# Seven quarter products in place of eight in a part of the first projection (retention attention followed by a snake MLP)

## The chip, the cores and the metric

The kernel runs on one core of a Trainium2 chip. The time is the device time of one execution in microseconds, and of several executions the median counts.

## The reference, cut to what matters

Eight batches of eight heads (576 positions, head size 64) go through a causal, decaying retention attention without softmax; its output, 4608 tokens of 512 features, goes through an MLP with a hidden layer of 2048.

```python
scores = scale * np.matmul(q, k.transpose(0, 1, 3, 2))
ret = scores * Dmat[None]                    # Dmat: gamma[h] ** (i - j) for i >= j, else 0
x = np.matmul(ret, v)                        # then as (4608, 512)
h = x @ w_in                                 # (4608, 512) @ (512, 2048)
s = np.sin(alpha * h)
g = h + s * s / (alpha + 1e-09)
return (g @ w_out).astype(np.float32)        # (4608, 2048) @ (2048, 512)
```

## The kernel before, in words

The tokens are taken in nine blocks `n` = 0 to 8 of 512. Blocks 0 to 7 hold the first 512 positions of batch `n`; block 8 holds the last 64 positions of all eight batches ("ends"). A block's input `xs[n]` lies transposed in SBUF (128 partitions, 4 chunks of the 512 features, 512 tokens); for block 8 it is `xS`, which class `Ends` makes while block 7 is projected.

**First projection.** The hidden layer is cut into 16 units of 128 features. `project(n, u, tag)` (line 560) is four matmuls 128x128x512 into one PSUM bank; units 4 to 7 take their weights from `w_in16[1]`, a tile whose columns are laid out so that a unit's 128 columns stand four apart. Then `sine` (573) on ScalarE reads the bank, `square` (581) is done on ScalarE or VectorE, and `product` (590) on VectorE reads the bank once more and writes `g = h + s²/alpha` to `gT[n]`. Only `product` gives the bank back. There are eight banks: `h0`, `h1`, `h2` go round (`next(h)`), `m0` and `m1` are double ones, also used by the attention, and `op` is for the second projection.

**Second projection.** From block 4 on it is already done with seven products in place of eight. For block `n-1` they are spread over the units of block `n`: behind units 1, 3, 5, ... stands one of `part_product(n-1, k)` (659), 16 matmuls 128x128x256, in the order 1, 2, 6, 7, 5, 3, 4. Products 2, 7 and 3 go into the bank of 1, 6 and 5: they are added to what lies there. So `after_product` (699), which reads the bank of 1, 6 or 5 (into `low`, `mid` or the output tile `osb`), must be done before TensorE may go on into it. The sums that these products take as factors are `row_sum` S1 to S4 (644, recorded at 652), VectorE instructions 128x1024 with both inputs in SBUF, half of them behind units 13 to 15 of block `n-1`, half behind units 0 to 2 of block `n`.

**Order.** All is issued under a manual schedule: each engine runs its instructions in the order of the program text, and TensorE, ScalarE, VectorE and GpSimd wait for each other by semaphores alone. `unit_start` records `project`, `sine` and what `at_unit(u, ...)` put there; then comes the part product, if any, then `unit_end` with `square`, `product` and what `behind(u, ...)` put there. `ON_V` names the units whose square is VectorE's. In block 7, `Ends` issues its scores at unit 7, its values at unit 13 and its results (`keep`, ScalarE and VectorE) behind it; a mark (`told`, 273), an empty instruction on GpSimd, stands between two halves of the values. GpSimd does the casts and state sums of the attention for the blocks before, and nothing in blocks 7 and 8 but such marks. `PAD` = 8 small loads (`fill_up`, 746) stand in SyncE's queue at units 3 to 10 of block 7.

## Time and profile before

| | us |
|---|---|
| median of 3 runs (lowest, highest) | 295.13 (293.91, 295.16) |
| the profiled execution | 293.87 |
| its span, first to last instruction | 292.1 |
| what lies around the span (293.87 less 292.1) | 1.77 |
| busy: TensorE matmul / VectorE / ScalarE / GpSimd | 282.4 / 228.7 / 206.2 / 135.8 |
| block 7's units, 221.3 to 249.6 of the span: VectorE / ScalarE / GpSimd busy | 24.7 / 20.2 / 0 |
| block 8's units, 249.6 to 277.4 of the span: VectorE / ScalarE / GpSimd busy | 23.3 / 17.6 / 0 |

In the profile's rows a line stands for the place in the kernel that recorded the instruction (L568 is `project`, L671 `part_product`, L576 `sine`, L585 ScalarE's and L587 VectorE's or GpSimd's `square`, L592 `product`, L652 `row_sum`, L702 to L717 `after_product`). PE is TensorE's matmul side, PEld its weight loads, DVE VectorE, ACT ScalarE, POOL GpSimd, SP SyncE. In a timeline the first two columns are start and length in us; `x8` merges eight instructions; a bracket at the end gives idle time before it and who ended it.

### The profile page before, as it was taken

To read this page: it belongs to the slowest core of one execution; us is meant where nothing else is said; L and a number is where in the kernel's file an instruction comes from. 1 tells how busy PE (TensorE), PEld (TensorE's weight loads), DVE (VectorE), ACT (ScalarE), POOL (GpSimd) and SP (SyncE) were. 2 spreads that over 40 slices of the span, in tenths; PEclk is the share of its full clock that TensorE was granted. 3 is DMA by queue.
4 is the path that set the end of the run, shared out by engine and by line. 5 is a ranking of instruction groups with operands and counts; after the bars stand their busy time and mean duration, and the time that the engine had idled before them with its cause. 6 is when DMAs were issued, how large, how long until landed. Compare 5 with 4: busy or idle time off the path is not lost. (4 is left out here: it accounts for less than half of the span.)

```text
span 292.1 us, 8463 instructions
## 1 busy us (share of the span) xinstructions
PE 282.4 (97%) x3480; PEld 182.9 (63%) x3480; DVE 228.7 (78%) x336; ACT 206.2 (71%) x340; POOL 135.8 (46%) x152
## 2 busy tenths in 40 slices
PE   5889999999999999999999999999999999999994
PEld 4656555555545645455776677676767676777783
DVE  2596969888659787798977697769777987987884
ACT  2588945997595887787767986897678657865500
POOL 6694777475699566560497039803960000000000
PEclk9599999999999999999999999999999999999999
DMA  7999999999999898999968985899651102111213
GB/s 211 349 235 209 242 289 317 263 262 258 226 220 188 169 159 180 274 164 180 156 154 236 133 206 144 245 137 221 167 159 43 43 10 80 36 38 36 72 38 108
DMA packets 122775, 50.06 MB, mean 171 GB/s; under 512 B 79729, under 2 KB 120689, under 8 KB 122737
## 3 DMA queue, kind: packets, MB, share of 16 engines
q1 hardware_dynamic: 118784, 44.76, 65.5%
q0 software_dynamic: 2688, 4.19, 7.9%
q10 hardware_dynamic: 1264, 0.58, 0.8%
q8 instruction: 27, 0.44, 0.6%
q14 instruction: 12, 0.09, 0.1%
HBM read 36.75 MB, written 9.44 MB: 158 GB/s over the span
## 5 line engine op out<-in xcount | busy, mean ns | idle before, releaser
L592 DVE SCALAR_TENSOR_TENSOR gT<-ss,inva,hps 128x512 f16<-128x512 f16 x144 | 105.6, 745 | 27.3 <-ACT ss L585 23.1
L576 ACT ACTIVATE s<-hps,alpha_t 128x512 f16<-128x512 f32 x144 | 96.4, 681 | 43.2 <-PE hps L568 42.4
L568 PE MATMUL hps<-xT,w_in 128*128 128x512 f16 (+1 forms) x532 | 121.4, 371 | 0.2
L568 PEld LDWEIGHTS <-w_in 128*128 128x128 f16 x596 | 66.7, 114 | 50.0 <-issue 1.0
L585 ACT ACTIVATE ss<-s 128x512 f16<-128x512 f16 x106 | 66.6, 630 | 2.8
L605 PE MATMUL ops<-w_out,gT 128*128 128x512 f16 x192 | 46.8, 380 | 0.0
L671 PEld LDWEIGHTS <-gT 128*128 128x128 f16 x384 | 37.5, 98 | 8.3
L207 POOL TENSOR_TENSOR k<-raw,cn 128x1024 f16<-128x1024 f32 (+1 forms) x17 | 28.8, 1698 | 10.2 <-DMA raw<-in_k_dram 8.7
L671 PEld LDWEIGHTS <-S 128*128 128x128 f16 x288 | 27.7, 98 | 5.3
L605 PEld LDWEIGHTS <-gT 128*128 128x128 f16 x192 | 17.9, 98 | 20.5
L363 POOL TENSOR_TENSOR s<-kvs,cn 128x256 f16<-128x256 f32 x17 | 10.4, 612 | 39.2 <-DVE S L652 24.8
L207 POOL TENSOR_TENSOR q<-raw,cn 128x1024 f16<-128x1024 f32 x13 | 25.1, 1938 | 4.9 <-DMA raw<-in_q_dram 4.6
L671 PE MATMUL hps<-T,gT 128*128 128x256 f16 x192 | 22.9, 273 | 0.0
L671 PE MATMUL hps<-w_out,gT 128*128 128x256 f16 x192 | 22.9, 273 | 0.0
L671 PE MATMUL hps<-w_out,S 128*128 128x256 f16 x192 | 22.8, 273 | 0.0
L401 DVE TENSOR_TENSOR ret<-sc,mask 128x1024 f16<-128x1024 f32 x16 | 19.2, 1220 | 2.6 <-PE sc L389 2.5
L120 ACT CAST xT<-o 128x1024 f16<-128x1024 f32 (+1 forms) x15 | 16.5, 1130 | 2.4 <-PE o L451 2.4
L587 DVE TENSOR_TENSOR ss<-s 128x512 f16<-128x512 f16 x29 | 14.9, 517 | 2.6 <-ACT s L576 2.5
L371 POOL TENSOR_TENSOR kvs<-s,kvs 128x256 f32<-128x256 f32 x21 | 15.3, 730 | 2.8 <-DVE kvs L122 1.2
L717 DVE TENSOR_TENSOR osb<-hps,low 128x512 f32<-128x512 f32 x13 | 9.0, 692 | 9.3 <-PE hps L671 9.2
L370 POOL TENSOR_TENSOR s<-kvs,cn 128x256 f32<-128x256 f32 x21 | 13.5, 642 | 5.9 <-ACT kvs L120 5.8
L652 DVE TENSOR_TENSOR S<-gT,S 128x1024 f16<-128x1024 f16 x24 | 15.6, 688 | 0.0
(83 smaller groups left out, 273.8 us busy)
## 6 DMA issues: line engine op xcount, KB each, us to landing
raw<-in_q_dram SPq DMA_DIRECT2D x16, 512.0 KB, 5.7
out_dram<-osb SPq DMA_DIRECT2D x32, 256.0 KB, 2.7
raw<-in_k_dram SPq DMA_DIRECT2D x8, 512.0 KB, 8.8
raw<-in_v_dram SPq DMA_DIRECT2D x8, 512.0 KB, 6.1
raw<-in_v_dram SPq DMA_DIRECT2D x32, 128.0 KB, 3.1
raw<-in_k_dram SPq DMA_DIRECT2D x32, 128.0 KB, 3.1
w_in<-in_moe_w_in_dram POOLq DMA_DIRECT2D x4, 512.0 KB, 11.7
w_out<-in_moe_w_out_dram POOLq DMA_DIRECT2D x4, 512.0 KB, 13.0
```

The source lines that it names most:

```text
L120: eng.copy(d_, s_)
L207: eng.tensor_tensor(dst[:, a0:a1].rearrange("p a r t d -> p t (a r) d"), t_.rearrange("p (t a) x -> p t a x", t=2)[:, :, a0:a1].rearrange( ...
L371: nc.gpsimd.tensor_tensor(self.kvs[:, c], s32, self.kvs[:, c], ADD)
L401: nc.vector.tensor_tensor(ret.rearrange("p t (z x) -> p (t z) x", z=2)[:, :, 0:n], sc.rearrange("p t (z x) -> p (t z) x", z=2)[:, :, 0:n], ...
L568: matmul(hps_of[n, fc][0][:, cols], w_in16[fc // 4][:, a, fc % 4 :: 4], xs[n][:, a, cols], start=(a == 0 and part != 1), stop=(a == KT - 1 ...
L576: nc.scalar.activation(s_t, hps, mybir.ActivationFunctionType.Sin, bias=0.0, scale=alpha_t[:, fc : fc + 1],)
L585: nc.scalar.activation(ss_t, s_t, mybir.ActivationFunctionType.Square)
L587: eng.tensor_tensor(ss_t, s_t, s_t, MULT)
L592: nc.vector.scalar_tensor_tensor(gT[n][:, fc, :], ss_t, inva[:, fc : fc + 1], hps, MULT, ADD)
L605: matmul(ops[n, c, cols.start][:, cols], gT[n][:, fk, c * P : (c + 1) * P], w_out16[:, fk, cols], start=(fk == 0), stop=(fk == FC - 1), sk ...
L652: return eng.tensor_tensor(out_, x, y, op)
L671: matmul(acc[:, 256 * j : 256 * j + 256], lhs[:, x, 128 * j : 128 * j + 128], rhs[:, x], start=(tag is not None and j == js[0] and p == 0 ...
```

## The change

Units 4 to 7 of blocks 7 and 8 are no longer four `project` calls. The 512 features of `w_in16[1]` are cut into two halves `t` (units 4 and 5, units 6 and 7), the 512 tokens into two halves `e`, and the 512 input features into two halves. Seven `sub_product`s of four matmuls 128x128x256 each (28 in all, where there were 16 of 128x128x512) give what eight quarter products gave. For this there are new sums:

- `w_in_sum` (recorded at line 754 of the changed kernel): S1 to S4 of the weights, once, eight GpSimd instructions 128x256 behind unit 14 of block 6.
- `x_sum` (769): T1 to T4 of the block's input, four GpSimd instructions 128x512 per block; for block 7 ahead of its units, for block 8 behind unit 14 of block 7.
- `after_sub` (795 to 806): products 1 and 2 are read by ScalarE, 6, 7, 5, 3 and 4 by VectorE, into `low_x`, `mid_x` and `hsb` in SBUF (float32). Products 2, 7 and 3 go into the bank of 1, 6 and 5 here too. Units 4 and 5 are whole after product 3, units 6 and 7 after product 4.
- The sine of the four units reads `hsb`. All four squares are ScalarE's; units 4 and 5 are ended by GpSimd with two instructions each (824, 825), units 6 and 7 by VectorE's `product`.
- `ON_V` goes from (3, 5, 9, 11) to (3,) in block 7 and from (3, 5, 7, 9, 11, 13) to (11, 13) in block 8. The eight `fill_up` loads move to units 3, 8, 9 and 10, two at each; `Ends`' scores stand among the products.

```diff
+    FIRST = {
+        1: ((0, 0), (0, 0)), 2: ((0, 1), (1, 0)), 3: ("S4", (1, 1)), 4: ((1, 1), "T4"),
+        5: ("S1", "T1"), 6: ("S2", "T2"), 7: ("S3", "T3"),
+    }
...
+    def w_in_sum(g, name, eng):
+        a11, a12, a21, a22 = (w_part(g, t, k_) for t in range(2) for k_ in range(2))
+        s_ = lambda x: w_sum_of(g, x)
+        x, y, op = {
+            "S3": lambda: (a11, a21, SUB), "S2": lambda: (a22, s_("S3"), SUB),
+            "S1": lambda: (a11, s_("S2"), ADD), "S4": lambda: (a12, s_("S2"), SUB),
+        }[name]()
+        for j in range(2):
+            eng.tensor_tensor(s_(name)[:, j], x[:, j], y[:, j], op)
...
+    def x_sum(n, name, eng):
+        b11, b12, b21, b22 = (x_part(n, k_, e) for k_ in range(2) for e in range(2))
+        t_ = lambda x: x_sum_of(n, x)
+        x, y, op = {
+            "T3": lambda: (b22, b12, SUB), "T2": lambda: (t_("T3"), b11, ADD),
+            "T1": lambda: (b12, b11, SUB), "T4": lambda: (b21, t_("T2"), SUB),
+        }[name]()
+        eng.tensor_tensor(t_(name), x, y, op)
+
+    def sub_product(n, g, i, tag, first=None):
+        left, right = FIRST[i]
+        accs[n, g, i] = accs[n, g, first] if tag is None else bank(tag)
+        acc = accs[n, g, i]
...
+        for j in range(2):
+            for a in range(2):
+                matmul(
+                    acc[:, 256 * j : 256 * j + 256], lhs[:, j, a], rhs[:, a],
+                    start=(tag is not None and j == 0 and a == 0), stop=(a == 1), skip_group_check=True,
+                )
+
+    def after_sub(n, g, i):
...
+        if i == 1:
+            nc.scalar.copy(low_, acc)
+        elif i == 6:
+            nc.vector.tensor_tensor(mid_, acc, low_, ADD)
+        elif i == 7:
+            nc.vector.tensor_tensor(low_, acc, low_, ADD)
+        else:
+            t, e = {2: (0, 0), 3: (0, 1), 4: (1, 0), 5: (1, 1)}[i]
+            dst = hs[t][:, :, 256 * e : 256 * e + 256]
+            if i == 2:
+                nc.scalar.copy(dst, as_pair(acc))
+            else:
+                nc.vector.tensor_tensor(dst, as_pair(acc), as_pair(mid_ if i == 3 else low_), ADD)
...
+    def product_on_pool(n, u):
+        hps, ss_t = hps_of.pop((n, u))
+        nc.gpsimd.tensor_tensor(ss_t, ss_t, inva[:, u : u + 1].to_broadcast([P, 512]), MULT)
+        nc.gpsimd.tensor_tensor(gT[n][:, u, :], ss_t, hps, ADD)
...
-            ON_V = {4: (), 5: (), 6: (0, 15), 7: (3, 5, 9, 11), 8: (3, 5, 7, 9, 11, 13)}[n]
+            ON_V = {4: (), 5: (), 6: (0, 15), 7: (3,), 8: (11, 13)}[n]
...
+            def opening(n, g):
...
+                sub_product(n, g, 1, next(h))
+                sub_product(n, g, 6, next(h))
+                after_sub(n, g, 1)
+                after_sub(n, g, 6)
+
+            def group(g, i, between, then):
+                part(slots[i])
+                for k_ in (2, 7, 5):
+                    sub_product(n, g, k_, next(h) if k_ == 5 else None, {2: 1, 7: 6}.get(k_))
+                    after_sub(n, g, k_)
+                for f in between:
+                    f()
+                part(slots[i + 1])
+                sub_product(n, g, 3, None, 5)
+                after_sub(n, g, 3)
+                sub_product(n, g, 4, next(h))
+                after_sub(n, g, 4)
+                for f in then:
+                    f()
...
+            plain_units(0, 2, units)
+            opening(n, 1)
+            group(1, 2, between, [E[1].masked] if n == 7 else [])
+            made = rest(1, (G_, V))
+            for f in (made[0], made[2], made[1], made[4]):
+                f()
+            at_unit(8, *made[6:8])
+            behind(8, *made[8:])
+            behind(8, made[3], made[5])
+            plain_units(4, 8, units)
```

(`rest` makes the list of sines, squares and ends of units 4 to 7; `plain_units` is the loop of before, two units and a part product at a time.)

**What stands where on VectorE in block 7.** Before, from the end of unit 4 (`ss_570`) to the output of part product 5 (the `osb` row): the rows L592 end units 4, 5, 6, 7 and 8 in turn, L704 and L706 read part products 6 and 7, L499 are the masks of `Ends`.

```order
L592 SCALAR_TENSOR_TENSOR gT<-ss_570,inva,hps 128x512
L704 TENSOR_TENSOR mid<-hps,low 128x512
L587 TENSOR_TENSOR ss_546<-s_544 128x512
L592 SCALAR_TENSOR_TENSOR gT<-ss_546,inva,hps 128x512
L592 SCALAR_TENSOR_TENSOR gT<-ss_548,inva,hps 128x512
L499 TENSOR_TENSOR rets<-scs,mask 128x1024
L706 TENSOR_TENSOR low<-hps,low 128x512
L592 SCALAR_TENSOR_TENSOR gT<-ss_532,inva,hps 128x512
L499 TENSOR_TENSOR rets<-scs,mask 128x1024
L592 SCALAR_TENSOR_TENSOR gT<-ss_570,inva,hps 128x512
L717 TENSOR_TENSOR osb<-hps,low 128x512
```

Now the same stretch from the reading of quarter product 7 on (its rows L797 and L704, for quarter product 6 and part product 6, stand just ahead). L806 are quarter products 5, 3 and 4; the three L592 end units 8, 6 and 7.

```order
L799 TENSOR_TENSOR low_x<-hps,low_x 128x512
L806 TENSOR_TENSOR hsb<-hps,low_x 128x2x256
L499 TENSOR_TENSOR rets<-scs,mask 128x1024
L706 TENSOR_TENSOR low<-hps,low 128x512
L806 TENSOR_TENSOR hsb<-hps,mid_x 128x2x256
L806 TENSOR_TENSOR hsb<-hps,low_x 128x2x256
L499 TENSOR_TENSOR rets<-scs,mask 128x1024
L592 SCALAR_TENSOR_TENSOR gT<-ss_570,inva,hps 128x512
L592 SCALAR_TENSOR_TENSOR gT<-ss_546,inva,hsb 128x512
L592 SCALAR_TENSOR_TENSOR gT<-ss_548,inva,hsb 128x512
L717 TENSOR_TENSOR osb<-hps,low 128x512
```

The ends of units 4 and 5 are gone from VectorE; between the ends of unit 8 and the output of part product 5 now stand the ends of units 6 and 7, with both tensors from SBUF.

**ScalarE in block 7.** Before, from the sine of unit 4 to that of unit 9 (L576 sine, L585 square):

```order
L576 ACTIVATE s_557<-hps,alpha_t 128x512
L585 ACTIVATE ss_570<-s_557 128x512
L576 ACTIVATE s_544<-hps,alpha_t 128x512
L576 ACTIVATE s_524<-hps,alpha_t 128x512
L585 ACTIVATE ss_548<-s_524 128x512
L576 ACTIVATE s_530<-hps,alpha_t 128x512
L585 ACTIVATE ss_532<-s_530 128x512
L576 ACTIVATE s_557<-hps,alpha_t 128x512
L585 ACTIVATE ss_570<-s_557 128x512
L576 ACTIVATE s_544<-hps,alpha_t 128x512
```

Now the copies of quarter products 1 and 2 and then ten instructions up to the square of unit 7 (L811 and L819 are the sines and squares of units 4 to 7, L576 the sine of unit 8, the three L585 the squares of units 8, 6 and 7):

```order
L795 COPY low_x<-hps 128x512
L804 COPY hsb<-hps 128x2x256
L811 ACTIVATE s_557<-hsb,alpha_t 128x512
L819 ACTIVATE ss_4368<-s_557 128x512
L811 ACTIVATE s_544<-hsb,alpha_t 128x512
L819 ACTIVATE ss_4371<-s_544 128x512
L576 ACTIVATE s_524<-hps,alpha_t 128x512
L811 ACTIVATE s_530<-hsb,alpha_t 128x512
L811 ACTIVATE s_557<-hsb,alpha_t 128x512
L585 ACTIVATE ss_570<-s_524 128x512
L585 ACTIVATE ss_546<-s_530 128x512
L585 ACTIVATE ss_548<-s_557 128x512
```

The first sine of the group moved from the end of unit 4's own matmuls to behind quarter product 3, and unit 8's square to behind seven others.

**GpSimd.** Where its program ended with the last cast of block 6, the difference adds the weight sums, the sums of block 7, the ends of units 4 and 5 of block 7, and the sums of block 8 (block 8's four ends follow):

```order
+L754 TENSOR_TENSOR S_w_4120<-w_in_1_71 128x256 x2
+L754 TENSOR_TENSOR S_w_4120<-w_in_1_71,S_w_4120 128x256 x2
+L754 TENSOR_TENSOR S_w_4125<-w_in_1_71,S_w_4120 128x256 x4
+L769 TENSOR_TENSOR T_x_4134<-xT_439 128x512
+L769 TENSOR_TENSOR T_x_4134<-T_x_4134,xT_439 128x512
+L769 TENSOR_TENSOR T_x_4137<-xT_439 128x512
+L769 TENSOR_TENSOR T_x_4137<-xT_439,T_x_4134 128x512
+L824 TENSOR_TENSOR ss_4368<-ss_4368,inva 128x512
+L825 TENSOR_TENSOR gT<-ss_4368,hsb 128x512
+L824 TENSOR_TENSOR ss_4371<-ss_4371,inva 128x512
+L825 TENSOR_TENSOR gT<-ss_4371,hsb 128x512
```

All of it is new; nothing of GpSimd's earlier rows moved.

More of the change, by code (lines that the diff above doesn't have):

```diff
@@ new lines, in part, with plain_units @@
+            def part(k_):
+                if k_ is not None:
+                    part_product(n - 1, k_, None if k_ in (2, 7, 3) else "op", first={2: 1, 7: 6, 3: 5}.get(k_))
+                    after_product(n - 1, k_)
+            def plain_units(i0, i1, units):
+                for i in range(i0, i1):
+                    for u in (2 * i, 2 * i + 1):
+                        unit_start(u, units[u], aside.get(u) or next(h))
+                        if u % 2:
+                            part(slots[i])
+                        if n < 8 and u == 14:
+                            square(n, u, A_)
+                            continue
+                        if n < 8 and u == 15:
+                            product(n, 14)
+                            for f in after.get(14, []):
+                                f()
+                        unit_end(u, units[u], None if A and u == 13 else V if u in ON_V else A_)
```

104 lines of the change are left out of this document (79 added, 25 removed).

## Prediction

> **What bounds the kernel now.** The page comes first: matmuls are busy for 97% of the span, no other engine over 78%.
>
> ```profile
> PE 282.4 (97%) x3480; PEld 182.9 (63%) x3480; DVE 228.7 (78%) x336; ACT 206.2 (71%) x340; POOL 135.8 (46%) x152
> ```
>
> That is a share over the whole program, so the second view is the busy time by stretch: block 7's units (first row) and block 8's (second).
>
> ```profile
> core 0: us, PE busy (x) PEld busy (x) DVE busy (x) ACT busy (x) POOL busy (x), PEclk, DMA share, GB/s
> 221.34:249.63 28.29, 28.26 (x370) 19.88 (x369) 24.73 (x38) 20.17 (x34) 0.00 (x0) 1.00 0.15 44
> 249.63:277.42 27.79, 27.79 (x195) 19.74 (x194) 23.26 (x38) 17.59 (x29) 0.00 (x0) 1.00 0.14 48
> ```
>
> In both TensorE works without a gap, at full clock: it sets the time, and nothing here can be won but matmul time. GpSimd is empty, VectorE and ScalarE have a few us each. So two questions decide: how much matmul time goes, and whether TensorE must now wait for somebody. The third view is TensorE's timeline, which gives the price of its pieces.
>
> ```profile
> 228.29 1.89 PE L568 MATMUL hps<-xT,w_in 128*128 128x512 f16 x8
> ...
> 235.98 1.89 PE L568 MATMUL hps<-xT,w_in 128*128 128x512 f16 x8
> 237.71 1.91 PE L671 MATMUL hps<-w_out,S 128*128 128x256 f16 x16
> 239.46 1.89 PE L568 MATMUL hps<-xT,w_in 128*128 128x512 f16 x8
> ...
> 256.58 1.89 PE L568 MATMUL hps<-xS,w_in 128*128 128x512 f16 x8
> ```
>
> A group's length holds the tail of its last matmul, so the price is start to start: two units 237.71 - 235.98 = 1.73 (one unit 0.87), a part product of 16 matmuls 239.46 - 237.71 = 1.75. Units 4 and 5 start at 228.29 in block 7 and at 256.58 in block 8.
>
> **Matmul time removed.** Four units, 4 x 0.87 = 3.46, go; 28 matmuls 128x128x256 come, 28/16 x 1.75 = 3.06 (one quarter product of four: 0.44). That is 0.40 a block, **0.80 in both**, 0.3% of the time. More than this can't be won, since there is no idle TensorE time to win.
>
> **What TensorE now waits for: the bank of part product 5.** Part product 3 goes into that bank, so it waits until VectorE has written `osb` from it (L717). In the changed order that row stands behind the ends of units 8, 6 and 7, which need ScalarE's squares, and these stand behind the sines and squares of units 4 and 5, which need quarter product 3. I add this chain up from ScalarE's rows (unit 8 and 9 of block 7) and VectorE's.
>
> ```profile
> 237.05 0.69 ACT L576 ACTIVATE s<-hps,alpha_t 128x512 f16<-128x512 f32 x1 [1.63 <-PE hps L568]
> 237.76 0.63 ACT L585 ACTIVATE ss<-s 128x512 f16<-128x512 f16 x1
> 238.30 0.67 ACT L576 ACTIVATE s<-hps,alpha_t 128x512 f16<-128x512 f32 x1
> ```
>
> ```profile
> 222.81 0.68 DVE L652 TENSOR_TENSOR S<-gT 128x1024 f16<-128x1024 f16 x1
> 223.41 0.42 DVE L587 TENSOR_TENSOR ss<-s 128x512 f16<-128x512 f16 x1
> ...
> 224.52 1.29 DVE L652 TENSOR_TENSOR S<-gT,S 128x1024 f16<-128x1024 f16 x2
> ...
> 228.25 0.75 DVE L592 SCALAR_TENSOR_TENSOR gT<-ss,inva,hps 128x512 f16<-128x512 f16 x1
> 228.90 1.29 DVE L652 TENSOR_TENSOR S<-gT,S 128x1024 f16<-128x1024 f16 x2
> 230.10 0.43 DVE L587 TENSOR_TENSOR ss<-s 128x512 f16<-128x512 f16 x1
> 230.57 1.40 DVE L592 SCALAR_TENSOR_TENSOR gT<-ss,inva,hps 128x512 f16<-128x512 f16 x2
> 231.96 0.69 DVE L704 TENSOR_TENSOR mid<-hps,low 128x512 f32<-128x512 f32 x1
> ...
> 247.88 1.28 DVE L122 CAST xS<-os 128x512 f16<-128x512 f32 x2
> ...
> 251.09 0.69 DVE L652 TENSOR_TENSOR S<-gT 128x1024 f16<-128x1024 f16 x1
> ...
> 252.35 1.29 DVE L652 TENSOR_TENSOR S<-gT,S 128x1024 f16<-128x1024 f16 x2
> ...
> 256.73 1.29 DVE L652 TENSOR_TENSOR S<-gT,S 128x1024 f16<-128x1024 f16 x2
> ```
>
> A square starts 0.71 after its own sine (237.76 - 237.05), the next instruction 0.54 after a square's start (238.30 - 237.76); for two independent instructions in a row I take 0.55 too. On VectorE an end (L592) takes 0.75 and the next starts 0.65 after it (1.40 for two), a reading of PSUM (L704) takes 0.69 and the next may start 0.61 after it. A reader starts 0.20 after TensorE has issued the last matmul (unit 8 is issued at 235.98 + 0.87 = 236.85, its sine starts at 237.05). Sines from SBUF, and readings into `hsb`, have no rows; I take them at these prices, since shape and types are the same. Zero is the start of quarter product 3:
>
> - 0.20 part product 7 can be read; 0.81 `hsb` of product 3 starts behind it, 1.50 it ends.
> - ScalarE: sine 4 at 1.50, square 2.21, sine 5 at 2.75, square 3.46, sines 8, 6, 7 at 4.00, 4.55, 5.10, squares 8, 6, 7 at 5.65, 6.20, 6.74. Square 8 ends at 6.28, square 7 at 7.37.
> - VectorE: end of unit 8 at 6.28, of 6 at 6.93, of 7 at 7.58, `osb` at 8.23 to 8.92.
> - TensorE meanwhile has quarter products 3 and 4, units 8 and 9, part product 5, units 10 and 11: 2 x 0.44 + 1.73 + 1.75 + 1.73 = 6.09.
>
> So part product 3 starts at 8.92 where TensorE is free at 6.09: **a wait of 2.83 in each block, 5.66 in both**. In block 7 most of it falls already on unit 11, which takes unit 8's bank: due at 5.22, released at 7.03. In block 8 the `m` banks take every third unit and only part product 3 waits. ScalarE's work before quarter product 3 can't start sooner, and VectorE's row can't be passed: each engine keeps its order.
>
> **At the front.** Quarter product 6 takes unit 2's bank. In block 7 TensorE comes there at 228.29 + 0.44 = 228.73; the end of unit 2 is done at 228.25 + 0.75 = 229.00: wait 0.27. Then 0.44, part product 6 (1.75) and quarter product 2 (0.44) bring it to 231.63 at product 7, which needs `mid_x` read. That stands behind the end of unit 3: 230.57 + 0.65 = 231.22, ends 231.91: wait 0.28. In block 8 the row sums end at 256.73 + 1.29 = 258.02, unit 3's end takes 0.65, `mid_x` is read at 259.36, and TensorE comes at 256.58 + 0.44 + 0.44 + 1.75 + 0.44 = 259.65: no wait, 0.29 to spare. **Front: 0.55.**
>
> **GpSimd's sums and ends.** They are new; the nearest rows are these (groups by shape), and its last cast in the timeline.
>
> ```profile
> L371 POOL TENSOR_TENSOR kvs<-s,kvs 128x256 f32<-128x256 f32 x21 | 15.3, 730 | 2.8 <-DVE kvs L122 1.2
> ...
> L363 POOL TENSOR_TENSOR s<-kvs,cn 128x256 f16<-128x256 f32 x17 | 10.4, 612 | 39.2 <-DVE S L652 24.8 <-PE hps L568 12.0 <-ACT kvs L120 1.8
> ...
> L191 POOL TENSOR_TENSOR ks<-ks,cn 128x512 f16<-128x512 f32 x2 | 2.1, 1042 | 1.8 <-PE o L430 1.8
> ```
>
> ```profile
> 215.71 0.61 POOL L122 CAST vs<-ends 128x512 f16<-128x512 f32 x1
> ```
>
> Eight weight sums at 0.61 run from 216.3 to 221.2, block 7's four x sums at 1.04 to 225.4: over 3 us before quarter product 6 needs T2, so TensorE waits for none of them. But they don't run alone: a place where GpSimd worked beside such VectorE rows is at 127 us.
>
> ```profile
> 127.21 1.04 POOL L191 TENSOR_TENSOR ks<-ks,cn 128x512 f16<-128x512 f32 x1 [1.77 <-PE o L430]
> ...
> 127.46 1.34 DVE L652 TENSOR_TENSOR gT<-gT 128x1024 f16<-128x1024 f16 x1
> ...
> 128.22 1.49 POOL L191 TENSOR_TENSOR qs<-qs,cn 128x512 f16<-128x512 f32 x1
> ...
> 128.73 1.26 DVE L587 TENSOR_TENSOR ss<-s 128x512 f16<-128x512 f16 x1
> ```
>
> There a row sum took 1.34 in place of 0.68 and a square 1.26 in place of 0.42: each, started while a GpSimd instruction ran, ended about as late as if it had begun at that one's end. In block 7, S2 (222.81), the square (223.41) and S1 (224.52) meet x sums. Each may lose from nothing to a whole GpSimd instruction, 1.04; I take half, 0.52, near the 0.66 of the row sum above: 3 x 0.52 = 1.56. VectorE has no gap from there to the end of unit 2, so TensorE waits that much more at quarter product 6. In block 8 the x sums run behind the casts, from 249.2 to 253.3, and meet S2 (251.09) and S1 (252.35): 1.04 less the 0.29 to spare, 0.75. **2.31 in both.**
>
> [...]
>
> GpSimd's ends of units 4 and 5 are four instructions 128x512 in float32, 0.73 (L371) plus what 256 more elements cost, 1.042 - 0.612 = 0.43: 4 x 1.16 = 4.64, from the end of square 4 (2.84 on the chain's clock) to 7.48. The ends of units 6 and 7 read `ss` and `hsb`, both in SBUF, as row sums and squares do; unit 6's, due at 6.93, would wait till 7.48: 0.55 a block, **1.10 in both**. At 0.73 each they would be through at 5.76 and cost nothing, at twice 0.73 they cost 1.75 a block.
>
> **The rest at nothing.** VectorE loses seven squares and four ends and gets ten readings; beside the named waits it has gaps. GpSimd's mark between the halves of `Ends`' values comes behind its ends: due at about 8.92 + 1.75 + 1.73 = 12.4 on the chain's clock, GpSimd is through at 7.5. SyncE's eight loads move behind units 3 and 8 to 10; a store may go out some us later, and four `osb` buffers cover that.
>
> **Sum.** -0.80 + 5.66 + 0.55 + 2.31 + 1.10 = +8.8. On the profiled execution, 293.87 (span 292.1 and 1.77 around it), this gives **302.7**; it lies 1.26 under the median of the runs shown, and a run may fall as far above.
>
> [...]
>
> **Rivals.**
> 1. *GpSimd's sums fall between VectorE's rows.* Then 2.31 and 1.10 go: -0.80 + 5.66 + 0.55 = +5.4, 299.3. For it: few places show such a cost. Against: VectorE has no gap from 222 to 234 us.
> 2. *Contention at full price*: x sums each hold a whole instruction (3.12 and 2.83 in place of 1.56 and 0.75 with a third meeting in block 8), ends 1.75 a block: +5.41 + 5.95 + 3.50 = +14.9, 308.7.
> 3. *No wait arises, not slower.* The place is the bank of part product 5: if the chain to `osb` took 6.09 in place of 8.92, TensorE would get there just in time, and the front waits would be all that stands against the 0.80: 293.87 - 0.80 = 293.1 to 293.6. It needs ten ScalarE instructions in 2.83 less than 5.87, half of their rows' prices. That quarter products cost more than 0.44 (weights four columns apart, at most a few hundredths each) moves the sum by far less.
>
> **How the numbers follow.** Forecast 0.58, rival 1 0.22, rival 2 0.15, rival 3 0.05. The time is the forecast's, 302.7. The range holds rival 1 and most of the way to rival 2: 298.9 to 308. Within 0.5% is about what a measurement of this kernel can tell from no change; slower by more 0.95, within 0.04, faster by more 0.01, since 0.80 is all that could be won.
>
> **What would show it.** In the profile after: part product 3 of blocks 7 and 8 starting right behind an `osb` row, with TensorE idle for 2 to 4 us in all before it; row sums and squares of over 1 us while L769 runs; ten ScalarE rows without a gap behind quarter product 3. It is wrong if TensorE stays without gaps there, or if the waits lie at quarter products, for GpSimd's T sums.

## The result, and the profile after

The changed kernel takes 309.49 us (median of 4 runs, 308.36 to 310.11) where the kernel before takes 294.62 beside it: a ratio of 1.052, with a 95% interval of 1.049 to 1.054. It is slower, as forecast, but by 15 us instead of 9: the forecast was 302.7, its range ended at 308.0. The profiled execution took 309.3, its span is 307.6.

Executions differ in their first 50 us, which the change leaves alone: in the profiles of this document block 7 starts anywhere from 221.1 to 227.2 us, and in three profiles of the changed kernel itself at 221.4, 223.9 and 226.2. Below I therefore compare the **stretch** from the start of block 7's units to the end of the span: 292.10 - 221.34 = 70.76 us before, 307.6 - 221.43 = 86.17 after. The difference, 15.41, is the whole loss.

The page's first part says that TensorE is busier than before and yet fills less of the span (93% where it was 97%), with 24 matmuls more.

```profile
PE 286.7 (93%) x3504; PEld 186.3 (61%) x3504; DVE 235.4 (77%) x335; ACT 211.8 (69%) x351; POOL 161.3 (52%) x176
```

The busy time by stretch says where the loss lies; these are block 7's and block 8's units in the changed kernel.

```profile
core 0: us, PE busy (x) PEld busy (x) DVE busy (x) ACT busy (x) POOL busy (x), PEclk, DMA share, GB/s
221.43:259.11 37.68, 31.10 (x383) 22.10 (x382) 28.57 (x38) 22.63 (x39) 11.89 (x12) 0.91 0.11 33
259.11:292.87 33.76, 29.31 (x206) 21.37 (x205) 25.06 (x37) 20.55 (x35) 9.63 (x8) 0.95 0.11 40
```

Block 7 went from 28.29 to 37.68, block 8 from 27.79 to 33.76. TensorE's busy time fell short of the stretch by 6.58 and 4.45, so it waits; but it was also busy *longer* than before (31.10 for 28.26, 29.31 for 27.79) although it has less to do, and the granted clock is 0.91 and 0.95 where it was 1.00. That second loss is in no term of the forecast. TensorE's timeline of block 7 shows both.

```profile
228.37 0.60 PE L779 MATMUL hps<-xT,w_in 128*128 128x256 f16 x4
232.31 1.01 PE L779 MATMUL hps<-T_x,S_w 128*128 128x256 f16 x4 [3.34 <-DVE gT L592]
233.12 3.62 PE L671 MATMUL hps<-T,S 128*128 128x256 f16 x16
236.53 1.06 PE L779 MATMUL hps<-xT,w_in 128*128 128x256 f16 x4
237.38 1.31 PE L779 MATMUL hps<-T_x,S_w 128*128 128x256 f16 x8
...
241.02 0.60 PE L779 MATMUL hps<-xT,S_w 128*128 128x256 f16 x4
...
245.37 1.03 PE L568 MATMUL hps<-xT,w_in 128*128 128x512 f16 x4
248.41 1.02 PE L568 MATMUL hps<-xT,w_in 128*128 128x512 f16 x4 [2.02 <-DVE gT L592]
250.66 1.91 PE L671 MATMUL hps<-w_out,S 128*128 128x256 f16 x16 [1.23 <-DVE osb L717]
```

```profile
core 0: us, PE busy (x), PEclk, DMA share, GB/s
...
233.12:236.53 3.41, 3.41 (x17) 0.50 0.05 10
...
237.38:238.62 1.24, 1.24 (x9) 0.78 0.00 0
250.66:252.40 1.74, 1.74 (x16) 1.00 0.49 160
282.75:285.93 3.18, 3.18 (x17) 0.53 0.23 82
```

TensorE stands 3.34 at quarter product 6, and behind it the 16 matmuls of part product 6 take 3.41 start to start (233.12 to 236.53) in place of 1.75: the clock is 0.50 there, and full again only past 238. The two waits at the back (2.02 before unit 11, 1.23 before part product 3) come as forecast, with the clock at 1.00 behind them. In block 8 the back is one wait, and the half clock follows it:

```profile
270.49 1.03 PE L779 MATMUL hps<-T_x,S_w 128*128 128x256 f16 x8 [0.93 <-DVE mid_x L797]
...
282.75 3.34 PE L671 MATMUL hps<-w_out,S 128*128 128x256 f16 x16 [3.41 <-DVE osb L717]
285.93 1.89 PE L568 MATMUL hps<-xS,w_in 128*128 128x512 f16 x8
```

Who is late at the front, VectorE's timeline of block 7 shows, beside GpSimd's x sums:

```profile
222.89 1.68 DVE L652 TENSOR_TENSOR S<-gT 128x1024 f16<-128x1024 f16 x1
224.49 1.37 DVE L587 TENSOR_TENSOR ss<-s 128x512 f16<-128x512 f16 x1
...
226.56 2.43 DVE L652 TENSOR_TENSOR S<-gT,S 128x1024 f16<-128x1024 f16 x2
...
231.43 0.73 DVE L592 SCALAR_TENSOR_TENSOR gT<-ss,inva,hps 128x512 f16<-128x512 f16 x1
```

```profile
222.87 1.15 POOL L769 TENSOR_TENSOR T_x<-xT 128x512 f16<-128x512 f16 x1
224.10 1.48 POOL L769 TENSOR_TENSOR T_x<-T_x,xT 128x512 f16<-128x512 f16 x1
225.54 1.33 POOL L769 TENSOR_TENSOR T_x<-xT 128x512 f16<-128x512 f16 x1
226.84 1.60 POOL L769 TENSOR_TENSOR T_x<-xT,T_x 128x512 f16<-128x512 f16 x1
```

The first S2 takes 1.68 (0.68 before), the square 1.37 (0.42), S1 and S4 together 2.43 (1.29; S1 0.86 and S4 1.64), each while an x sum runs: +1.00, +0.95 and +1.14, in sum 3.09. The end of unit 2, which gives quarter product 6 its bank, starts at 231.43 in place of 228.25.

**The account.** All in us, start to start, against 0.44 for a quarter product, 1.75 for a part product and 1.73 for two units:

| | forecast | block 7 | block 8 |
|---|---|---|---|
| matmul time removed | -0.40 a block | -0.40 | -0.40 |
| front waits (quarter products 6 and 7) | 2.11 / 0.75 | 3.50 | 0.28 + 1.09 = 1.37 |
| half clock behind a wait | none | 0.37 + 1.66 + 0.41 + 0.37 = 2.81 | 3.18 - 1.75 = 1.43 |
| back waits (unit 11, part product 3) | 2.83 + 0.55 = 3.38 a block | 9.64 - 6.09 = 3.55 | 9.65 - 6.09 = 3.56 |
| sum | | 9.46 (measured 9.39) | 5.96 (measured 5.97) |

(9.64 is from quarter product 3 to part product 3, 241.02 to 250.66.) The start and the tail add 0.05. The forecast missed 6.6: the half clock 4.24, the front 1.39 and 0.62, the back 0.35.

### The profile page after: what moved, and what is told of

Same layout as the page of the kernel before. It is cut to its first block, busy times and chain, and to the rows that moved or that the text cites. A ratio compares the mean times of both kernels' runs of the same rounds, so it can differ in the third digit from the quotient of the medians.

```text
span 307.6 us, 8561 instructions
## 1 busy us (share of the span) xinstructions
PE 286.7 (93%) x3504; PEld 186.3 (61%) x3504; DVE 235.4 (77%) x335; ACT 211.8 (69%) x351; POOL 161.3 (52%) x176
## 5 line engine op out<-in xcount | busy, mean ns | idle before, releaser
L592 DVE SCALAR_TENSOR_TENSOR gT<-ss,inva,hps 128x512 f16<-128x512 f16 x136 | 99.4, 743 | 32.1 <-ACT ss L585 28.1
L568 PE MATMUL hps<-xT,w_in 128*128 128x512 f16 (+1 forms) x516 | 117.8, 371 | 2.8 <-DVE gT L592 2.0
L576 ACT ACTIVATE s<-hps,alpha_t 128x512 f16<-128x512 f32 x136 | 91.1, 681 | 34.9 <-PE hps L568 34.5
L568 PEld LDWEIGHTS <-w_in 128*128 128x128 f16 x564 | 63.0, 114 | 50.4 <-issue 3.1
L585 ACT ACTIVATE ss<-s 128x512 f16<-128x512 f16 x109 | 68.1, 630 | 2.7
L671 PEld LDWEIGHTS <-S 128*128 128x128 f16 x288 | 29.1, 103 | 11.5 <-issue 5.2
L671 PE MATMUL hps<-w_out,S 128*128 128x256 f16 x192 | 24.2, 283 | 4.6 <-DVE osb L717 4.6
L824 POOL TENSOR_TENSOR ss<-ss,inva 128x512 f32<-128x512 f32 x4 | 4.2, 1042 | 27.5 <-ACT ss L819 27.5
L652 DVE TENSOR_TENSOR S<-gT,S 128x1024 f16<-128x1024 f16 x24 | 17.9, 783 | 0.0
```

The costliest lines, as they stand in the source:

```text
L568: matmul(hps_of[n, fc][0][:, cols], w_in16[fc // 4][:, a, fc % 4 :: 4], xs[n][:, a, cols], start=(a == 0 and part != 1), stop=(a == KT - 1 ...
L576: nc.scalar.activation(s_t, hps, mybir.ActivationFunctionType.Sin, bias=0.0, scale=alpha_t[:, fc : fc + 1],)
L585: nc.scalar.activation(ss_t, s_t, mybir.ActivationFunctionType.Square)
L592: nc.vector.scalar_tensor_tensor(gT[n][:, fc, :], ss_t, inva[:, fc : fc + 1], hps, MULT, ADD)
L652: return eng.tensor_tensor(out_, x, y, op)
L671: matmul(acc[:, 256 * j : 256 * j + 256], lhs[:, x, 128 * j : 128 * j + 128], rhs[:, x], start=(tag is not None and j == js[0] and p == 0 ...
```

## Experiments

The theory that I took to the chip: (a) GpSimd's sums hold VectorE's rows with two inputs in SBUF for all that is left of a sum; (b) the late ends hold the `osb` row and so the bank of part product 5; (c) a TensorE wait of some 3.3 us or more brings the half clock behind it, whatever caused the wait. The rivals: the quarter products themselves are slow (weights four columns apart, more weight loads); or the slow matmuls come from something other than the wait.

### The sums left out

The w and x sums are dropped, and the quarter products multiply plain quarters, so the output isn't the reference's.

```diff
-        1: ((0, 0), (0, 0)), 2: ((0, 1), (1, 0)), 3: ("S4", (1, 1)), 4: ((1, 1), "T4"),
-        5: ("S1", "T1"), 6: ("S2", "T2"), 7: ("S3", "T3"),
+        1: ((0, 0), (0, 0)), 2: ((0, 1), (1, 0)), 3: ((0, 1), (1, 1)), 4: ((1, 1), (1, 0)),
+        5: ((0, 0), (0, 1)), 6: ((1, 1), (1, 1)), 7: ((1, 0), (0, 1)),
...
-                    behind(14, lambda nm=nm: w_in_sum(1, nm, G_))
...
-                    x_sum(7, nm, G_)
...
-                    behind(14, lambda nm=nm: x_sum(8, nm, G_))
```

> The changed kernel with GpSimd's sums left out: the quarter products take plain quarters of the weights and of the input in place of S1 to S4 and T1 to T4, so units 4 to 7 of blocks 7 and 8 are not the reference's. All else stays, GpSimd's ends of units 4 and 5 too. Theory (GpSimd's sums hold up VectorE's two-input rows, and a TensorE wait of over 3 us halves its clock): in block 7 the S2, square and S1/S4 rows take 0.68, 0.42 and 1.29 again in place of 1.68, 1.37 and 2.43; quarter product 6 waits about 0.3 in place of 3.34; the clock stays at 1.00 there; block 7 gets about 5.7 shorter, block 8 about 1.1, the time 302.5. Rival (the quarter products themselves, with weights four columns apart and 28 in place of 16, are what is slow): wait or clock at the front stay, time above 307.

Measured: 307.9, stretch 82.12. VectorE's rows in this run:

```profile
225.54 0.68 DVE L652 TENSOR_TENSOR S<-gT 128x1024 f16<-128x1024 f16 x1
226.15 0.42 DVE L587 TENSOR_TENSOR ss<-s 128x512 f16<-128x512 f16 x1
...
227.26 1.29 DVE L652 TENSOR_TENSOR S<-gT,S 128x1024 f16<-128x1024 f16 x2
```

and TensorE's:

```profile
231.78 0.60 PE L779 MATMUL hps<-xT,w_in 128*128 128x256 f16 x4 [0.15 <-DVE gT L592]
232.21 1.91 PE L671 MATMUL hps<-T,S 128*128 128x256 f16 x16
...
245.46 1.02 PE L568 MATMUL hps<-xT,w_in 128*128 128x512 f16 x4 [2.02 <-DVE gT L592]
247.71 3.26 PE L671 MATMUL hps<-w_out,S 128*128 128x256 f16 x16 [1.23 <-DVE osb L717]
250.77 2.25 PE L568 MATMUL hps<-xT,w_in 128*128 128x512 f16 x8
```

(a) holds: the three rows are back at their own length, and the front wait of 3.34 is 0.15, with the next 16 matmuls at 1.75. But the time missed its mark (block 7 got 3.93 shorter in place of the expected 5.7, block 8 0.11 in place of 1.1): the half clock, gone from the front, now stands behind the waits of 2.02 and 1.23 (247.71 to 250.77, 3.06 for 1.75), which brought none in the first profile, and in block 8 it lasts longer (280.10 to 283.46, 3.36 for 1.75, and the two units behind take 2.80 for 1.73). The wait was removed and the clock's loss came up elsewhere.

### The ends spread

Sines, squares and ends of units 4 to 7 are issued behind units 8 to 12, a few each, where they all stood ahead of unit 8's end before.

```diff
-            for f in (made[0], made[2], made[1], made[4]):
-                f()
-            at_unit(8, *made[6:8])
-            behind(8, *made[8:])
-            behind(8, made[3], made[5])
+            behind(8, made[0])
+            behind(9, made[2], made[1], made[3])
+            behind(10, made[4], made[6], made[5])
+            behind(11, made[8], made[7], made[9])
+            behind(12, *made[10:])
```

> The changed kernel with sines, squares and ends of units 4 to 7 spread over units 8 to 12, each behind a unit's own rows, in place of all around unit 8. Theory (part product 3 waits because the output of part product 5 stands behind eight ScalarE rows): the waits before unit 11 and part product 3 (2.02 and 1.23 in block 7, 3.41 in block 8) go or fall below 0.5, with block 8's the half clock behind it; the front stays as it is (3.34 and half clock); together 8.5 less, 300.8. Rival (ScalarE and VectorE have no room for this work, it only waits elsewhere): the waits come back at later units, less than 4 us gained, above 305.

Measured: 302.46, 1.7 more than I expected, stretch 79.64. (b) holds: no wait is left before unit 11 and part product 3 in either block, and block 8's half clock went with its wait. The front kept its 3.34 and its half clock (16 matmuls in 2.71). New waits came with the later ends: 1.01 before unit 15, 0.88 before block 8 (VectorE's `keep` rows for `xS`), 0.67 at quarter product 7 of block 8, 0.94 in the tail.

### Both together

The two edits above in one kernel (sums left out, ends spread).

> The changed kernel without the w and x sums (the quarter products multiply plain quarters, so the output is not the reference's) and with the sines, squares and ends of units 4 to 7 spread behind units 8 to 12. Theory (contention at the front, the late osb row, and the half clock behind either, are the whole loss): what is left against the kernel before is the 0.80 us won and the small waits that the spread ends made, 0.15 at the front, 1.01 before unit 15, 0.88 before block 8, 0.94 in the tail, so the stretch from block 7's start to the span's end is 70.76 - 0.80 + 2.98 = 72.9 us, with every group of 16 matmuls at 1.75. Rival (the quarter products or their readings cost something of their own): 75 or more, with long groups or waits at the quarter products.

Measured: 297.5, stretch 74.55, 3.79 above the kernel before. Every wait with a bracket of over 1.1 us is gone, and so is the half clock (mean granted clock 1.000). It is 1.65 more than I expected, for a reason in my reading: a bracket counts idle time from the end of the last matmul, which lies about 0.2 behind the point at which the next could have started, so each of these waits costs about 0.2 more than its bracket; and two part products near the end, part way through for VectorE's late rows, took 2.01 and 2.05. Added up start to start, the waits are 0.31, 1.20, 1.04, 0.26, 0.30 and 1.10; less 0.80 that is 3.4 of the 3.79. Most of the rest is a wait without a bracket at quarter product 7 of block 7 (quarter products 2, 7 and 5 take 1.70 there before the next matmul starts, 231.14 to 232.84, in place of 1.31), where the prediction had 0.28. No quarter product itself is slow.

### Idle matmuls in the two long waits

The changed kernel, with 10 matmuls on zeros ahead of quarter product 6 in block 7 and 14 ahead of part product 3 in block 8. They fill the waits and end none.

```diff
+                if n == 7:
+                    keep_busy(10, "m0")
...
+                            if n == 8 and i == 5:
+                                keep_busy(14, "m0")
```

> The changed kernel with idle matmuls 128x128x512 on a zero tile put into the two long waits: 10 ahead of quarter product 6 in block 7, 14 ahead of part product 3 in block 8. No wait is taken away. Theory (the clock falls because TensorE did nothing for over 3 us): the clock stays at 1.00 in both places, the 16 matmuls behind them take 1.75 again in place of 3.41 and 3.18, and the time falls by about 4.2 to 305. Rival (the rows behind the waits are slow for another reason: weights not loaded ahead, banks, the sums' tiles): they stay at twice their length, and the time stays at 309 or rises.

Measured: 312.82, but block 7 starts at 227.21 here; the stretch is 83.89, 2.28 less than 86.17.

```profile
235.48 2.32 PE L835 MATMUL idle<-zero 128*128 128x512 f16 x10 [0.72 <-DVE gT L592]
238.09 0.60 PE L779 MATMUL hps<-T_x,S_w 128*128 128x256 f16 x4 [0.30 <-DVE gT L592]
238.53 1.91 PE L671 MATMUL hps<-T,S 128*128 128x256 f16 x16
...
251.68 1.02 PE L568 MATMUL hps<-xT,w_in 128*128 128x512 f16 x4 [2.02 <-DVE gT L592]
253.94 3.51 PE L671 MATMUL hps<-w_out,S 128*128 128x256 f16 x16 [1.23 <-DVE osb L717]
257.29 1.89 PE L568 MATMUL hps<-xT,w_in 128*128 128x512 f16 x8
```

The delay up to quarter product 6 is the same (3.49 from where TensorE could start), yet part product 6 takes 1.74: it isn't the product or its factors that were slow, but the clock after idle time. The same in block 8 (1.75 behind the filled wait). Of the 4.24 saved so, 1.60 came back: the waits of 2.02 and 1.23, which I had not filled, brought the half clock this time (3.35 for 1.75). Another 0.21 is a wait at quarter product 7 of block 7.

### A long wait in the kernel before

No quarter products at all: the kernel before, with eight more VectorE readings of part product 5's bank in block 8 (their results are used by nothing). Then the same with five.

```diff
+                        if n == 8 and k_ == 5:
+                            more_ = work.tile([P, 512], F32, tag="ret0", bufs=1, name="more")
+                            for _ in range(8):
+                                nc.vector.tensor_tensor(more_, parts[n - 1, k_], kept["low"], ADD)
```

> The kernel before, without any quarter product, with eight more readings of part product 5's bank on VectorE in block 8, ahead of its output: a wait of TensorE of about 4.3 us before part product 3 (8 readings of 0.61 to 0.69, less 0.8 of slack) and nothing else. Theory (a wait over 3 us halves the clock, whoever makes it): the 16 matmuls of part product 3 show a clock of about 0.5 and take over 3 us; time before plus 4.3 plus 1.4 to 1.8, about 300. Rival (half clock belongs to the quarter products): clock 1.00, time before plus 4.3, about 298.5.

> The kernel before with five more VectorE readings of part product 5's bank in block 8 (their result is used by nothing), so TensorE has one wait there that is about 3 x 0.61 shorter than the 4.73 us of the run with eight: 2.9 us. The stretch from the start of block 7 to the end of the span was 70.76 us in the kernel before and 77.76 with eight readings. Theory (TensorE's clock falls only when it has stood idle long enough, some 3.3 us or more in the runs so far): the 16 matmuls behind the wait take 1.75 as before and the stretch is 70.76 + 2.9 = 73.7. Rival (any wait of over 2 us brings the half clock): the 16 matmuls take over 3 us and the stretch is about 75.4.

Measured with eight: 301.3, stretch 77.76, 7.00 above the kernel before. With five: 298.52, stretch 73.48, 2.72 above. First eight, then five:

```profile
274.11 3.57 PE L671 MATMUL hps<-w_out,S 128*128 128x256 f16 x16 [4.73 <-DVE osb L717]
277.48 2.28 PE L568 MATMUL hps<-xS,w_in 128*128 128x512 f16 x8
```

```profile
273.42 1.91 PE L671 MATMUL hps<-w_out,S 128*128 128x256 f16 x16 [2.55 <-DVE osb L717]
275.16 1.89 PE L568 MATMUL hps<-xS,w_in 128*128 128x512 f16 x8
```

(c) holds without any of the change's work. A wait of 4.73 costs 4.89 start to start, and 2.00 more behind it: 3.37 for 1.75, then 2.11 for 1.73, at a granted clock of 0.50 and 0.82. A wait of 2.55 costs 2.71 and nothing behind it. Three readings more or less (1.83 of VectorE's time) make 4.28 of difference. Each is one execution; that the length alone decides is not shown by these two, and the next section says what else does.

### The changed kernel again, twice

> The changed kernel once more, unaltered. The idle stretches of TensorE at part product 3 of block 7 (2.02 ahead of unit 11 and 1.23 ahead of the part product) left the clock at 1.00 here, but brought the half clock behind the same two waits in the run without sums and in the run with filled waits. Theory (whether the clock falls behind waits of about 3.3 us depends on where they fall in time, not on the kernel): the front of block 7 (one wait of 3.3 us) shows some loss again, and the place at part product 3 of block 7 may show 16 matmuls of over 3 us in one of these two executions. Rival (the kernel alone decides): both executions repeat the first, with 3.4 us for the 16 matmuls of part product 6 in block 7, 1.75 at part product 3 there, 3.2 at part product 3 of block 8, and a stretch of 86.2 us within 0.2.

> The changed kernel a third time; the same two theories as for the second: by the first, the 16 matmuls behind the three waits of about 3.3 us take anything from 1.75 to 3.4 us, differently in the three executions; by the rival, they take 3.4, 1.75 and 3.2 in each.

Measured: 310.72 and 314.68, stretches 85.15 and 86.76. The waits are the same to 0.03 in all three executions; the half clock behind them isn't. The 16 matmuls behind the three places (front of block 7; unit 11 and part product 3 of block 7; part product 3 of block 8) took 3.41, 1.75, 3.18 in the first, 2.83, 1.75, 3.12 in the second, 2.91, 3.22, 3.17 in the third. The second place in the third execution:

```profile
252.02 1.02 PE L568 MATMUL hps<-xT,w_in 128*128 128x512 f16 x4 [2.02 <-DVE gT L592]
254.28 3.39 PE L671 MATMUL hps<-w_out,S 128*128 128x256 f16 x16 [1.24 <-DVE osb L717]
```

So the kernel decides the waits, and something else, which differs between two executions on one chip, decides part of what the clock makes of them.

The granted clock, read from the traces in slices of 0.1 us, shows what that is. In the first execution of the changed kernel it falls at 231.11, comes back at 237.93, falls at 282.31 and comes back at 285.72: 2, 15 and 16 steps of 3.413 us behind the first point; the two stretches at half clock last 6.83 and 3.41, two steps and one. In the kernel before it falls at 8.34, comes back at 15.16 and falls at 291.64, 2 and 83 such steps behind the first. So I take the points at which it can change as a grid with a step of 3.413. In the second execution the clock falls for the front wait only at 235.74, when TensorE has been at work again for 1 us. Cut into windows at the points of its own grid, each execution shows how busy TensorE was in a window, and the clock that followed:

| window | execution | what lies in it | TensorE busy | clock in the next window |
|---|---|---|---|---|
| 227.69 to 231.11 | changed, first | front wait | 38% | 0.50 |
| 228.91 to 232.33 | changed, second | front wait, first part | 73% | 1.00 |
| 232.33 to 235.74 | changed, second | front wait, rest | 30% | 0.50 |
| 244.76 to 248.17 | changed, first | wait of 2.02, first part | 48% | 1.00 |
| 248.17 to 251.59 | changed, first | rest of it, and 1.23 | 57% | 1.00 |
| 250.52 to 253.94 | changed, third | most of 2.02, and 1.23 | 30% | 0.50 |
| 244.66 to 248.07 | sums left out | most of 2.02, and 1.23 | 40% | 0.50 |
| 268.01 to 271.42 | before, eight readings | wait of 4.73, first part | 40% | 0.50 |
| 268.33 to 271.74 | before, five readings | wait of 2.55, first part | 74% | 1.00 |
| 271.74 to 275.15 | before, five readings | wait of 2.55, rest | 51% | 1.00 |

In this table the clock fell behind the windows in which TensorE was busy for 30 to 40%, and behind none of 48 to 74%. The whole traces of the kernel before and of the changed kernel, from the clock's first record on, agree: it fell behind windows at full clock that were busy for 0 and 33% (before, 288.23 to 291.64 and 4.92 to 8.34) and for 13, 21 and 38% (changed), and behind none of 48% or more. It came back behind windows at half clock that were busy for 84% (changed, second), 87% (changed, first) and 91% (before), and not behind those of 21% (eight readings), 62% (sums left out), 65% (changed, first) and 78% (before). So (c) was right that idle time brings the half clock, whoever makes it, and wrong that a length of some 3.3 us decides: in these executions the idle share of a window tells the falls from the rest, and the place of the grid, which lies differently in each, decides how a wait is cut. The wait of 2.55 was cut into 0.87 and 1.68; that it cost nothing does not make its length safe.

### The whole computation without the named costs

First repair: w sums on GpSimd a block earlier; x sums on VectorE (T3 and T2 ahead of a block's units, T1 and T4 among the quarter products); all ends on VectorE and spread; two squares (unit 15 of block 6, unit 3 of block 7) moved from VectorE to ScalarE, and three (units 9 and 11 of block 7, unit 9 of block 8) to VectorE.

```diff
-            if n == 6:
+            if n == 5:
                 for nm in ("S3", "S2", "S1", "S4"):
                     behind(14, lambda nm=nm: w_in_sum(1, nm, G_))
...
-                for nm in ("T3", "T2", "T1", "T4"):
-                    x_sum(7, nm, G_)
+                for nm in ("T3", "T2"):
+                    x_sum(7, nm, V)
...
-            made = rest(1, (G_, V))
...
+            made = rest(1, (V, V))
+            s4, s5, q4, g4, q5, g5, s6, s7, q6, g6, q7, g7 = made
+            behind(8, s4)
+            behind(9, q4, s5)
+            behind(10, g4, q5, s6)
+            behind(11, g5, q6, s7)
+            behind(12, g6, q7, g7)
```

> The whole computation, with the named costs taken away: w sums on GpSimd one block earlier, where VectorE is idle; x sums on VectorE, two in gaps before each block's units and two among the quarter products; ends of units 4 to 7 spread behind units 8 to 12 and all on VectorE; two squares moved from VectorE to ScalarE ahead of the quarter products. Theory (no wait is long enough for the half clock, no row of VectorE is held by GpSimd): by the rows' prices TensorE waits about 0.5 for T1, 0.9 before block 8 and 0.8 among block 8's quarter products, less the 0.80 won: about +1.4, a stretch of 72.2 us and a time 1.4 above the kernel before. Rival (VectorE has no room for 2.5 us of x sums and two more ends a block, and its queue ends in one long wait): a wait of over 3 us with the half clock behind it, a stretch of 76 or more.

Measured: 297.62, stretch 74.05, 3.29 above the kernel before where I expected 1.4. The clock is 1.000, no VectorE row is held (S2 0.68, S1 and S4 1.29). What stays are five small waits: 0.49 at quarter product 6 (T3 and T2 did not go into VectorE's gap but behind it), 0.24 and 0.33 for T1, 0.94 before block 8, 0.94 in the tail, each about 0.16 more start to start, and 0.26 without a bracket at quarter product 7 of block 8 (261.46 to 262.16 for 0.44). The second repair takes up the five:

```diff
+            if n == 6:
+                behind(13, lambda: x_sum(7, "T3", V), lambda: x_sum(7, "T2", V))
+            if n > 6:
+                behind(2, lambda: x_sum(n, "T1", G_), lambda: x_sum(n, "T4", G_))
...
-                    behind(13, lambda i=i: E[i // 2].keep(i % 2, V if i // 2 else A_))
+                    behind(13, lambda i=i: E[i // 2].keep(i % 2, A_))
...
+            behind(8, s4, s5, q4)
+            behind(9, s6, q5, g4)
+            behind(10, s7, g5, q6)
+            behind(11, g6, q7)
+            behind(12, g7)
```

> The whole computation; as in the run before, and the waits left there (0.49 at the front of block 7, 0.94 before block 8, 0.24 and 0.33 at quarter product 5, 0.94 in the tail) each taken up: T3 and T2 of block 7 in VectorE's idle 1.79 ahead of the last osb row of block 6; T1 and T4 of both blocks on GpSimd, behind the row sums, where VectorE only reads PSUM; all four keep rows on ScalarE; the ends one unit earlier, with the squares of units 8, 9 and 10 or 11 and of unit 4 on VectorE. Theory (all of the loss was waits, and the quarter products cost no more than their matmuls): TensorE stands nowhere by the rows' prices, and what is left is the 0.80 us won: a ratio of 0.997, a time of 293.2 where the kernel before has 294.0; with every price 3% higher 0.2 us of it goes, with 6% all of it. Rival (the sums, ends and readings fill VectorE and ScalarE too far): waits of 0.3 to 1 us stay at the quarter products, before block 8 or in the tail, and the time is 1 to 3 us above the kernel before.

Measured: 293.95 (12 runs, 293.17 to 296.13) beside 294.07 for the kernel before, a ratio of 0.999 with an interval of 0.996 to 1.003. That is no difference that these runs can tell. The profile can: block 7 and block 8 in this kernel,

```profile
222.90:250.79 27.89, 27.89 (x382) 20.94 (x381) 26.75 (x43) 21.13 (x37) 2.27 (x2) 1.00 0.15 45
250.79:278.18 27.39, 27.39 (x206) 20.83 (x205) 25.05 (x41) 20.22 (x35) 2.27 (x2) 1.00 0.14 48
```

are 27.89 and 27.39 long where they were 28.29 and 27.79: 0.40 less each, as priced, and TensorE is busy all through. The stretch is 70.10, 0.66 under the kernel before (the tail is 0.14 longer). The gain is real in the profile and smaller than what startup does to a run. GpSimd's T1 and T4 stand beside VectorE rows that read PSUM:

```profile
231.47 1.16 POOL L769 TENSOR_TENSOR T_x<-xT 128x512 f16<-128x512 f16 x1 [13.60 <-DVE S L652]
232.58 1.16 POOL L769 TENSOR_TENSOR T_x<-xT,T_x 128x512 f16<-128x512 f16 x1
```

```profile
231.90 0.68 DVE L797 TENSOR_TENSOR mid_x<-hps,low_x 128x512 f32<-128x512 f32 x1
232.66 0.69 DVE L704 TENSOR_TENSOR mid<-hps,low 128x512 f32<-128x512 f32 x1
233.54 0.69 DVE L799 TENSOR_TENSOR low_x<-hps,low_x 128x512 f32<-128x512 f32 x1 [0.18 <-PE hps L779]
```

Neither side is longer there: L704 took 0.69 in the kernel before too, and the shortest x sum of the changed kernel took 1.15. All four sums, beside VectorE's row sums and a square, had cost it 3.09; these two cost it nothing here.

## Why the prediction was wrong, step by step

- **Matmul time removed, 0.40 a block: right.** The second repair shows it bare: 28.29 - 27.89 and 27.79 - 27.39.
- **The wait for part product 5's bank: right in place, cause and size.** Quarter product 3 to part product 3 was forecast at 8.92, with the ends' hold 9.47; it took 9.64 and 9.65. In block 7 most of it fell on unit 11, as said. ScalarE's rows do run without a gap there; spreading the ends ended the wait. VectorE's rows of block 7 show what was late by more than the chain said: the end of unit 8 at 247.61, 0.31 after its mark (6.28 behind 241.02), since sines from SBUF took 0.70 to 0.72 for 0.68 and each step of ScalarE a little more, and then the ends of units 6 and 7.

```profile
247.61 0.75 DVE L592 SCALAR_TENSOR_TENSOR gT<-ss,inva,hps 128x512 f16<-128x512 f16 x1 [3.37 <-ACT ss L585]
248.28 1.73 DVE L592 SCALAR_TENSOR_TENSOR gT<-ss,inva,hsb 128x512 f16<-128x512 f16 x2
249.94 0.68 DVE L717 TENSOR_TENSOR osb<-hps,low 128x512 f32<-128x512 f32 x1
```

- **GpSimd's ends, 0.55 a block: too much by 0.2.** The two ends took 1.73 in place of 1.40, 0.33 more.
- **GpSimd's sums: the mechanism right, the size wrong.** "Each may lose from nothing to a whole GpSimd instruction, 1.04; I take half, 0.52": the three rows of block 7 lost 1.00, 0.95 and 1.14, the whole. (The last is a pair; its S1 lost 0.2 and its S4, which began 0.5 behind the start of the last sum, nearly all of it.) The four sums stand back to back, and S2 and the square too began 0.02 and 0.39 behind the start of a sum and ended about when they would have, had they begun at its end. Half is right for a row that meets one sum at a random moment; why each of these came so early in a sum is my reading of the rows (VectorE, once let go, holds up the next sum in turn: 1.33 to 1.60 for 1.15), not tested. 1.56 should have been 3.1, rival 2's price for these meetings. In block 8 S2 lost 0.41 and S1 and S4 1.25, and the wait was 1.37 for 0.75.
- **What failed: the sum counts a wait of TensorE at its own length.** No term and no rival of the prediction has the clock in it, though PEclk stood in the rows that it quoted. The half clock cost 4.24 of the 6.6 missed. The chain is: held rows made the front wait 3.50 in place of 2.11, and it, like the 3.56 of block 8, left TensorE busy for a small part of a window of 3.413 (38 and 13%), behind which the clock fell. The experiments bear it out: idle matmuls took the loss away at an unchanged delay, a wait without quarter products made it, and in blocks 7 and 8 no kernel in which every window was busy for 51% or more showed it (before, five readings, both edits together, both repairs). How much of it comes in one execution is a matter of where the grid lies: 1.3 to 2.8 at the front, nothing to 1.7 at the back of block 7.
- **Rival 2's 308.7 came near 309.3 by accident.** Its price for block 7's sums was right, 3.12; its 2.83 in block 8 and 1.75 a block for the ends did not occur, and together they stood in for the clock.

The forecast's own waits were 2.83 to 3.38 a block. The front wait of 3.31 to 3.34 brought the half clock in all four executions that had it, the 2.02 and 1.23 at the back of block 7 in three of five, and the forecast should have had the clock as a rival at 1 to 3 us for each place.

## What to carry over

Price an idle stretch of TensorE twice: its length, and the half clock that may follow. In these runs the clock fell behind a window of 3.413 us in which TensorE was busy for 40% or less, so about 2 us of idle time within one window (0.6 x 3.413, an estimate from these shares), in one wait or in two close together, can cost 1 to 3 us more; whether it does depends on where the window lies, so several executions are needed to see it. Where GpSimd has several instructions in a row, a VectorE row with two inputs in SBUF can lose nearly the whole of one at each meeting (0.95 and 1.00 of 1.15 here); put such sums beside rows that read PSUM (0.68 and 0.69 beside 1.16 here), or into VectorE's gaps. When a long and fully packed TensorE loses a multiplication, the gain is its matmul time at most (0.3% here), and the schedule around it has to have room for the sums, ends and readings before that is seen.

## What the runs showed of the hardware

- In the traces the granted clock changed at points that lie whole steps of 3.413 us apart, elsewhere in each execution. Of the windows given above it fell behind all that were busy for 40% or less and behind none of 48% or more; it came back behind those of 84% or more and behind none of 78% or less. None lay between 40 and 48%, so what happens there stays open.
- So the clock's loss depends on how the grid cuts a wait: the same two waits of 2.02 and 1.23, with 1.02 of matmuls between them, cost nothing in two executions of the changed kernel and 1.5 in the third (3.22 for 1.75); behind the front's 3.3 the loss was 1.3 to 2.8.
- Removing one wait does not remove the clock's loss in proportion: without sums the front's 2.8 went, but 1.7 came at the back of block 7, and block 8's 1.4 became 2.7, since the clock stayed down there for two windows in place of one.
- Startup varies more than the whole gain: block 7 began at 221.1 to 227.2 us in these runs. In the latest of them TensorE was busy for 40.7 of the first 50 us, at a granted clock of 0.90, against 44.3 at 1.00 in the first profile of the changed kernel. The clock isn't all of it: in the kernel before it was 0.93 there, and block 7 began at 221.3. What else varies was not looked into.
- What exactly is counted as busy stays open: the shares are the profile's, in which the end of a group of matmuls is modelled and lies some 0.16 late (1.89 for two units that are 1.73 apart).
